# Small spacer loads ahead of each whole-tile store in a group normalization kernel

## The chip, the cores and the metric

The kernel runs on one core of one Trainium2 chip. The metric is device time in microseconds (us). Most executions agree within 0.3%. The kernel before takes 634.3 us.

Names: PE is the matmul engine, DVE VectorE, ACT ScalarE, POOL GpSimd, SP SyncE. SP does no arithmetic here: it issues nearly all DMA transfers. The transfers are carried out by 16 DMA engines; of the 128 packets of a tile, one per partition, each engine has 8. Its packets wait in its queue, also called its ring. A semaphore is a counter that one engine raises and another waits for.

## The reference

Group normalization over `x` of shape 128 x 1024 x 32 x 16 in bf16, with 32 groups, then a scale and a shift per channel:

```python
def reference(x, g, b):
    G = 32
    B, C, H, W = x.shape[0], x.shape[1], x.shape[2], x.shape[3]
    xr = x.reshape(B, G, C // G, H, W)
    mu = xr.mean(axis=(2, 3, 4), keepdims=True)
    var = ((xr - mu) ** 2).mean(axis=(2, 3, 4), keepdims=True)
    xn = (xr - mu) / jnp.sqrt(var + 1e-5)
    xn = xn.reshape(B, C, H, W)
    return xn * g[None, :, None, None] + b[None, :, None, None]
```

All of `x` has to be read once and all of the output written once: 134 MB each way.

## The kernel before

`x` is cut into 32 tiles of 128 partitions (4 images x 32 groups) by 16384 bf16, which is 32 KB per partition and 4 MB per tile. Six tiles are held on the chip. A tile is loaded, its mean comes from PE and DVE, its squares from ACT, then DVE, POOL and ACT scale it in place, and it is stored from the same buffer. The parts that matter here are the transfers, all on SP's queue:

```python
XBUFS = 6
UPFRONT = 6
AHEAD = 5
STORE_IN_PARTS = 2
...
    def L(i):                                    # load of tile i
        xt = xpool.tile([P, F], BF16, name="xt")
        parts = NQ if i == 0 or i >= NT - 1 else 1
        ...
            chain("sp", nc.sync.dma_start(out=xt[...], in_=x_v[i][...]))

    for i in range(min(UPFRONT, NT)):            # six loads at once
        L(i)
...
    def S(i, lo, hi):                            # store of tile i
        chain("sp", nc.sync.dma_start(
            out=o_v[i][:, lo * QF : hi * QF],
            in_=state[i]["xt"][:, lo * QF : hi * QF]))
...
    def finish(i):
        if i < 0 or in_parts(i):                 # the last two tiles are stored in quarters
            return
        for k in range(KC - LAST_SHARE, KC):
            scale_on("act", i, k)
        S(i, 0, NQ)
        state.pop(i)
        j = i + AHEAD
        if UPFRONT <= j < NT:
            L(j)                                 # waits until the store of tile i - 1 has landed
```

`chain` keeps the order on an engine. In steady state SP therefore issues, once per tile: a load as soon as an earlier store has freed a buffer, then the next store.

Of the kernel before, what the change touches and what calls it, by code (L numbers as in the profile page):

```python
# [11 lines left out]
BF16 = mybir.dt.bfloat16  # L12
# [10 lines left out]
STORE_IN_PARTS = 2  # L23
ACT_SHARE = 2
LAST_SHARE = 3
POOL_SHARE = 13


@with_exitstack
def kernel(  # L30
# [13 lines left out]
    nc = tc.nc  # L44
    P = nc.NUM_PARTITIONS
# [6 lines left out]
    NT = B0 // NS  # L52
# [11 lines left out]
    x_v = x.rearrange("(t n) (g k) h w -> t (n g) (k h w)", n=NS, g=G)  # L64
# [5 lines left out]
    xpool = ctx.enter_context(tc.tile_pool(name="xpool", bufs=XBUFS))  # L70
    jpool = ctx.enter_context(tc.tile_pool(name="jpool", bufs=1))
    spool = ctx.enter_context(tc.tile_pool(name="spool", bufs=4))
    pspool = ctx.enter_context(
        tc.tile_pool(name="pspool", bufs=2, space=bass.MemoryType.PSUM)
    )
# [9 lines left out]
    def chain(key, inst):  # L85
        prev = last.get(key)
        if prev is not None:
            tc.add_manual_dep(inst.ins, prev.ins.name, nosync, reason="pipeline order")
        last[key] = inst
        return inst  # L90
# [16 lines left out]
    for i in range(min(UPFRONT, NT)):  # L107
# [14 lines left out]
        out=eye[:],  # L122
        in_=ones_b[:],
# [8 lines left out]
        out=rep[:].rearrange("q (n a) -> q n a", n=NS),  # L132
        in_=ones_b[0:G, :].rearrange("q (n a) -> q n a", n=NS),
# [223 lines left out]
    def scale_on(key, i, k):  # L357
        st = state[i]
        span = st["xt"][:, k * HW : (k + 1) * HW]
        scl = st["scl"][:, k : k + 1]  # L360
        bia = st["bia"][:, k : k + 1]
        if key == "act":
            inst = nc.scalar.activation(  # L363
                out=span, in_=span, func=ACT.Identity, bias=bia, scale=scl
            )
        else:
            eng = nc.vector if key == "dve" else nc.gpsimd
            inst = eng.tensor_scalar(  # L368
                out=span,
                in0=span,  # L370
                scalar1=scl,
                scalar2=bia,
                op0=ALU.mult,
                op1=ALU.add,
            )
        chain(key, inst)

    def S(i, lo, hi):
        chain(
            "sp",  # L380
            nc.sync.dma_start(
                out=o_v[i][:, lo * QF : hi * QF],
                in_=state[i]["xt"][:, lo * QF : hi * QF],
            ),
        )

    def in_parts(i):
        return i >= NT - STORE_IN_PARTS

    def A(i):  # L390

        if not in_parts(i):
            for n in range(POOL_SHARE):
                scale_on("pool", i, KC - LAST_SHARE - POOL_SHARE + n)
            for k in range(KC - LAST_SHARE - POOL_SHARE):
                scale_on("dve", i, k)
            if i + 1 < NT:
                R1(i + 1)
            return
        for c in range(NQ):  # L400
            for k in range(c * KQ, (c + 1) * KQ):
                on_act = i == NT - 1 and k >= (c + 1) * KQ - ACT_SHARE
                scale_on("act" if on_act else "dve", i, k)
            S(i, c, c + 1)
            if c == NQ // 2 - 1 and i + 1 < NT:
                R1(i + 1)

    def finish(i):
        if i < 0 or in_parts(i):
# [7 lines that stand above are left out]
            L(j)  # L417
# [42 lines left out]
```

## Time and profile before

| | before |
|---|---|
| time | 634.33 us (634.23 to 634.92, 3 runs) |
| DMA, 60 to 560 us | share 1.00, 430 to 432 GB/s |
| ACT, the busiest compute engine | 85% of the span |
| load, store: issue to landing (medians) | 29.3, 38.3 us |
| a load and a store issued every | 19.4 us |

The page of the kernel before: the busy time of each engine; then the DMA's busy tenths in 40 equal slices of the span, the GB/s of those slices and the number of packets; then the DMA issues (transfer, engine, count, KB each, median us from issue to landing).

```profile
PE 293.1 (46%) x1025; PEld 114.4 (18%) x1025; DVE 380.2 (60%) x645; ACT 539.0 (85%) x268; POOL 346.8 (55%) x523
...
DMA  8999999999999999999999999999999999999996
GB/s 365 431 437 423 430 431 429 431 433 431 424 430 432 431 431 429 430 433 438 428 432 429 433 431 429 430 430 433 434 431 431 430 430 432 433 426 436 433 418 271
DMA packets 11063, 268.70 MB, mean 425 GB/s; under 512 B 1312, under 2 KB 1312, under 8 KB 1312
...
xt<-in_x_dram SPq DMA_DIRECT2D x30, 4096.0 KB, 29.3
out_dram<-xt SPq DMA_DIRECT2D x30, 4096.0 KB, 38.3
```

The strip of nines is the main reading: the DMA engines are busy in every slice but the ends, while no compute engine is. The busy time by window says the same of two inner stretches; its columns are the window, its length, then busy time and count of PE, PEld, DVE, ACT and POOL, the clock granted to PE, the DMA share and GB/s.

```profile
60.00:300.00 240.00, 111.30 (x386) 43.07 (x384) 159.00 (x256) 224.06 (x107) 151.60 (x226) 0.72 1.00 430
300.00:560.00 260.00, 120.55 (x416) 46.63 (x416) 160.81 (x259) 224.60 (x106) 155.61 (x232) 0.71 1.00 432
```

A busy DMA could still be short of work now and then. SP's timeline (start, length, engine, line, operation) and its longest waits (us in total, times, longest) show that it is not:

```profile
240.62 0.34 SPq L101 DMA_DIRECT2D xt<-in_x_dram  x1
241.06 0.37 SPq L381 DMA_DIRECT2D out_dram<-xt  x1
260.36 0.34 SPq L101 DMA_DIRECT2D xt<-in_x_dram  x1
260.81 0.37 SPq L381 DMA_DIRECT2D out_dram<-xt  x1
```
```profile
SPq L101 <- DMA out_dram<-xt: 425.4, 26, 19.0
SPq L381 <- DVE xt L368: 151.7, 18, 38.6
```

The load issued at 240.62 lands 29.4 us later (the median is 29.3), though its own 4 MB take 9.7 us: the load and the store issued one round earlier stand ahead of it, and land at 250.6 and 260.3. So in steady state about 20 us of work is queued. The 425 us that SP waits for stores to land is back-pressure from a full queue, not a loss.

The trace also records each DMA packet. A partition's 32 KB row of a tile is one packet. The records do not name the engine; packets that follow each other without a gap are taken to be of one. On one engine such packets start 1209 to 1210 ns apart, so 16 engines make 433 GB/s. After the eight packets of a tile comes one 4-byte packet that raises the semaphore, about 6 ns. All packets of the kernel add up to about 620 us per engine (480 x 1209.5 + 128 x 306 + 76 x 6 ns); the rest of the 632 us span is the start, stalls inside packets, and the tail.

### The profile page before, as it was taken

To read this page: it belongs to the slowest core of one execution; us is meant where nothing else is said; L and a number is where in the kernel's file an instruction comes from. 1 tells how busy PE (TensorE), PEld (TensorE's weight loads), DVE (VectorE), ACT (ScalarE), POOL (GpSimd) and SP (SyncE) were. 2 spreads that over 40 slices of the span, in tenths; PEclk is the share of its full clock that TensorE was granted. 3 is DMA by queue.
4 is the path that set the end of the run, shared out by engine and by line. 5 is a ranking of instruction groups with operands and counts; after the bars stand their busy time and mean duration, and the time that the engine had idled before them with its cause. 6 is when DMAs were issued, how large, how long until landed. Compare 5 with 4: busy or idle time off the path is not lost.

```text
span 631.9 us, 3907 instructions
## 1 busy us (share of the span) xinstructions
PE 293.1 (46%) x1025; PEld 114.4 (18%) x1025; DVE 380.2 (60%) x645; ACT 539.0 (85%) x268; POOL 346.8 (55%) x523
## 2 busy tenths in 40 slices
PE   5578604553245633456433565335553345647000
PEld 2233201221112211122111222112221112213000
DVE  1087666666676576545775457754657654577660
ACT  4589999999999897877997779977989797797960
POOL 0077666666666576544775446764557654477100
PEclk9689758766787657876678766677865788658655
DMA  8999999999999999999999999999999999999996
GB/s 365 431 437 423 430 431 429 431 433 431 424 430 432 431 431 429 430 433 438 428 432 429 433 431 429 430 430 433 434 431 431 430 430 432 433 426 436 433 418 271
DMA packets 11063, 268.70 MB, mean 425 GB/s; under 512 B 1312, under 2 KB 1312, under 8 KB 1312
## 3 DMA queue, kind: packets, MB, share of 16 engines
q1 hardware_dynamic: 10944, 268.44, 99.0%
q8 instruction: 8, 0.13, 0.1%
q14 instruction: 15, 0.12, 0.0%
q10 hardware_dynamic: 96, 0.00, 0.0%
HBM read 134.22 MB, written 134.22 MB: 425 GB/s over the span
## 4 chain that ended last, share of the span: by engine, by line
DMA 67%; ACT 15%; PE 7%; issue 4%; DVE 3%; POOL 0%; SPq 0%; DVEq 0%; ACTq 0%; POOLq 0%
DMA out_dram<-xt 42%; DMA xt<-in_x_dram 25%; ACT ja L244 13%; PE pa L166 7%; DVE xt L368 3%; ACT xt L363 2%; DMA gb_b<-in_g_dram 1%; POOL scl L337 0%; SPq L101 0%; ACT rstd L308 0%; DVE rstd L312 0%; DVE jd L189 0%; POOL shift L343 0%; DVEq L455 0%; DVE bia L324 0%
## 5 line engine op out<-in xcount | busy, mean ns | idle before, releaser
L244 ACT ACTIVATE ja<-xt,negmean 128x8192 fp8e5<-128x8192 bf16 x60 | 426.7, 7112 | 52.1 <-DVE jd L189 52.0
L166 PE MATMUL pa<-xt,eye 128*128 128x512 bf16 x976 | 281.8, 460 | 289.7 <-DMA xt<-in_x_dram 278.5
L368 DVE TENSOR_SCALAR xt<-xt,scl,bia 128x512 bf16<-128x512 bf16 x536 | 352.6, 732 | 40.0 <-POOL bia L353 40.0
L368 POOL TENSOR_SCALAR xt<-xt,scl,bia 128x512 bf16<-128x512 bf16 x390 | 308.7, 806 | 3.4 <-POOL bia L353 0.3
L166 PEld LDWEIGHTS <-eye 128*128 128x128 bf16 x1024 | 114.3, 114 | 468.5 <-DMA xt<-in_x_dram 290.6
L337 POOL TENSOR_SCALAR scl<-gb,rstd 128x32 f32<-128x32 f32 x31 | 11.2, 361 | 218.2 <-DVE rstd L312 218.2
L189 DVE TENSOR_SCALAR_CACHE_REDUCE jd<-pa 128x512 bf16<-128x512 f32 x32 | 22.0, 688 | 149.0 <-PE pa L166 149.0
L363 ACT ACTIVATE xt<-xt,bia,scl 128x512 bf16<-128x512 bf16 x98 | 72.0, 798 | 0.8 <-DVE bia L324 0.8
L244 ACT ACTIVATE ja<-xt,q 128x4096 fp8e5<-128x4096 bf16 x8 | 29.6, 3706 | 6.6 <-DVE jd L189 6.4
L312 DVE RECIPROCAL rstd<-rstd 128x1 f32<-128x1 f32 x32 | 5.1, 160 | 35.8 <-ACT rstd L308 35.8
L343 POOL TENSOR_SCALAR shift<-scl,negmean 128x32 f32<-128x32 f32 x31 | 11.2, 360 | 3.1
L216 POOL TENSOR_SCALAR off<-negmean,q 128x1 f32<-128x1 f32 x2 | 0.9, 432 | 20.5 <-DVE jd L189 20.5
L166 PE MATMUL pb<-xt,eye 128*128 128x512 bf16 x48 | 11.6, 388 | 1.0 <-DMA xt<-in_x_dram 1.0
L308 ACT ACTIVATE rstd<-s,v 128x1 f32<-128x1 f32 x30 | 8.8, 294 | 2.8
L244 ACT ACTIVATION_READ_ACCUMULATOR ja<-xt,negmean 128x1 f32 x60 | 11.2, 187 | 0.0
L353 POOL TENSOR_TENSOR bia<-shift,gb 128x32 f32<-128x32 f32 x31 | 7.8, 252 | 2.6
L308 ACT ACTIVATE rstd<-var,eps_t 128x1 f32<-128x1 f32 x2 | 0.6, 295 | 9.2 <-DVE jv L292 9.2
L273 POOL TENSOR_SCALAR v<-s 128x1 f32<-128x1 f32 x30 | 5.8, 192 | 2.5
L156 DVE COPY gb<-gb_p 128x64 f32<-128x64 f32 x1 | 0.2, 224 | 5.6 <-PE gb_p L148 5.6
L116 ACT ACT_TABLE_LOAD x1 | 1.3, 1283 | 1.7 <-PEq L444 1.7
L189 DVE DVE_READ_ACCUMULATOR jd<-pa 128x1 f32 x32 | 2.6, 81 | 0.0
L292 DVE TENSOR_SCALAR_CACHE_REDUCE jv<-sq,seed 128x4 f32<-128x4 f32 x2 | 0.4, 216 | 2.7 <-ACT ja L244 2.7
(18 smaller groups left out, 6.1 us busy)
## 6 DMA issues: line engine op xcount, KB each, us to landing
xt<-in_x_dram SPq DMA_DIRECT2D x30, 4096.0 KB, 29.3
out_dram<-xt SPq DMA_DIRECT2D x30, 4096.0 KB, 38.3
xt<-in_x_dram SPq DMA_DIRECT2D x8, 1024.0 KB, 16.5
out_dram<-xt SPq DMA_DIRECT2D x8, 1024.0 KB, 17.8
gb_b<-in_g_dram ACTq DMA_DIRECT2D x1, 2.0 KB, 3.2
gb_b<-in_b_dram ACTq DMA_DIRECT2D x1, 2.0 KB, 5.3
```

What stands on the lines that cost most here:

```text
L116: chain("act", nc.scalar.activation(out=warm[:], in_=eps_t[:], func=ACT.Sqrt))
L166: nc.tensor.matmul(out=ps[:], lhsT=eye[:], rhs=st["xt"][:, k * MMN : (k + 1) * MMN], start=(k == lo), stop=(k == hi - 1),),
L189: nc.vector.tensor_scalar(out=jd[:], in0=ps[:], scalar1=-inv_n, scalar2=seed, op0=ALU.mult, op1=ALU.add, accum_out=total[:],),
L244: nc.scalar.activation(out=ja[:, 0:w], in_=st["xt"][:, k * w : (k + 1) * w], func=ACT.Square, bias=bias, scale=scale, accum_out=sq, satura ...
L273: nc.gpsimd.tensor_scalar(out=v0[:], in0=s0[:], scalar1=inv_n, scalar2=EPS, op0=ALU.mult, op1=ALU.add,),
L308: nc.scalar.activation(out=rstd[:], in_=last_sum[:], func=ACT.Sqrt, bias=bias[:], scale=scale),
L312: chain("dve", nc.vector.reciprocal(out=rstd[:], in_=rstd[:]))
L337: nc.gpsimd.tensor_scalar(out=scl[:], in0=gam, scalar1=rstd[:], scalar2=None, op0=ALU.mult),
L343: nc.gpsimd.tensor_scalar(out=shift[:], in0=scl[:], scalar1=st["negmean"][:], scalar2=None, op0=ALU.mult,),
L353: nc.gpsimd.tensor_tensor(out=bia[:], in0=shift[:], in1=bet, op=ALU.add),
L363: inst = nc.scalar.activation(out=span, in_=span, func=ACT.Identity, bias=bia, scale=scl)
L368: inst = eng.tensor_scalar(out=span, in0=span, scalar1=scl, scalar2=bia, op0=ALU.mult, op1=ALU.add,)
```

## The change

The intent can be read from the names: a spacer in the queue between a load and the store behind it. The spacer is a load of 64 bytes per partition into a small spare buffer that nobody reads.

```diff
+GAP = 32
...
+    gappool = ctx.enter_context(tc.tile_pool(name="gappool", bufs=4))
...
+    def spacer():
+
+        room = gappool.tile([P, GAP], BF16, name="room")
+        chain("sp", nc.sync.dma_start(out=room[:], in_=x_v[0][:, 0:GAP]))
+
     def S(i, lo, hi):
+        if i < NT - STORE_IN_PARTS:
+            spacer()
         chain(
             "sp",
             nc.sync.dma_start(
```

It makes 30 more transfers, for tiles 0 to 29. The built program differs on SP alone. One side effect is not in the diff: the framework hands eight semaphores round among the transfers, and a transfer that gets a semaphore must wait until that semaphore's previous transfer has landed. With two transfers per tile a semaphore returns after four tiles; with three, after 2.7.

## The prediction

> **What bounds the kernel.** The DMA queue. In the page's 40-slice strip DMA is 9 except at both ends; the stage table (busy time by window) gives 430 to 432 GB/s from 60 to 600 us, while ACT, the busiest engine, has 85% of the span. The Trainium skill ("DMA: Bandwidth & Descriptors", Where 436 GB/s comes from) states a ceiling of 435.2 GB/s; the trace agrees: in its DMA packet records a 32 KB packet lasts 1213 ns and the next on that engine starts after about 1210, so 16 engines make 433 GB/s. A whole tile is 8 such packets per engine and one semaphore packet (about 6 ns), 9.68 us. All 76 transfers sum to about 619 us of packet time; the rest of the 632 us span is start, stalls and tail.
>
> The queue never runs dry. The timeline of SP shows a load and a store issued together every 19.4 us; the issue table has loads landing 29.3 and stores 38.3 us after issue (medians), so some 20 us of work is always queued. SP's 425 us of waiting for stores to land is back-pressure. Even the last store quarter, issued at 614.3 us, lands 17 us later.
>
> **What the change does.** Nothing on the compute engines. It adds 30 DMAs (tiles 0 to 29) of 128 packets of 64 bytes: 8 packets and one semaphore packet per DMA engine, between a load and a store in steady state.
> - Issue: 0.34 us each on SP, hidden by the backlog.
> - Semaphores: eight are handed round; with three DMAs per tile each returns after 2.7 tiles, not 4. In the built order a store now also waits for the load of two periods before, 39 us old and landed at 29: slack 10 us. In the tail, stores 27 and 28 wait some 5 us longer, with over 15 us still queued. No cost.
> - Engine time: the Trainium skill (same page, Queues, rings and completion order) says that each DMA engine consumes descriptors in ring order; the trace agrees (landings 9.7 us apart in issue order). So the packets are paid in full. 64-byte packets of the small loads on ACT's queue last 11 ns in the trace, semaphore packets 9 at a pitch of 6. Estimate: 8 x 8 + 6 = 70 ns per spacer, 2.1 us for 30. If their reads overlap badly, perhaps 0.3 us each, 9 us.
> - Stalls: time over 1213 ns in 32 KB packets totals 2.7 us per engine on average, about 6.5 on the worst, 1.9 of the 2.7 in the last two packets of a transfer, mostly loads just before a store; engines end between 623.4 and 630.5 us. A spacer could reduce this, at best by 3 to 5 us on the slowest engine; it may do nothing.
>
> **Prediction.** 634.3 + 2.1 + about 0.6 for imperfect overlap, stalls either way: 637 us, range 632 to 644. Faster by over 2% 0.01 (it would nearly go under the packet time), same 0.91, slower by over 2% 0.08.
>
> **Right if** DMA stays 9 in every inner slice, packets rise by 4320 (3840 of 64 bytes, 480 of 4), landings grow apart by about 0.1 us per spacer, compute groups keep their times and SP still waits mainly for stores to land.
>
> **Wrong if** small reads are exposed one after the other (0.5 us or more per spacer, 15 us and up), if semaphore reuse empties the queue (DMA slices below 9), or if the spacing removes stalls at load-to-store borders (mean 32 KB packet below 1218.7 ns, last landing earlier).

## The result, and the profile after

The changed kernel takes 636.27 us (635.68 to 636.66, 4 runs) against 634.35 us (634.23 to 634.92, 4 runs). The ratio is 1.0029, with a 95% interval from 1.0015 to 1.0043. A ratio here is the mean time of one kernel's runs over that of the other's of the same rounds, so it is not quite the ratio of the medians. The change costs 1.9 us by the medians (1.0 to 2.7 by the interval). That is far under 2%.

The page of the changed kernel, the same parts as before, with the issues of the spacer:

```profile
PE 285.6 (45%) x1005; PEld 113.1 (18%) x1025; DVE 379.2 (60%) x645; ACT 539.0 (85%) x268; POOL 345.4 (54%) x523
...
DMA  9999999999999999999999999999999999999995
GB/s 372 440 431 407 427 430 431 430 430 430 420 431 434 432 430 431 431 434 438 429 430 431 430 430 430 435 429 433 430 432 431 436 430 437 434 414 436 435 413 236
DMA packets 15383, 268.95 MB, mean 424 GB/s; under 512 B 5632, under 2 KB 5632, under 8 KB 5632
...
xt<-in_x_dram SPq DMA_DIRECT2D x30, 4096.0 KB, 29.3
out_dram<-xt SPq DMA_DIRECT2D x30, 4096.0 KB, 38.2
...
room<-in_x_dram SPq DMA_DIRECT2D x30, 8.0 KB, 29.1
```

There are 15383 - 11063 = 4320 more packets, all of them small: 30 x (128 + 16). (PE's busy time is no finding: some matmul records are missing, 1005 of 1025.) The spacer lands 29.1 us after its issue although it is tiny: it waits its turn in the ring, behind the load. The queue is as full as before. The busy time by window, and SP's timeline and waits:

```profile
60.00:300.00 240.00, 108.71 (x378) 42.58 (x384) 158.01 (x255) 223.99 (x108) 150.71 (x226) 0.73 1.00 429
300.00:560.00 260.00, 116.72 (x407) 46.21 (x416) 158.25 (x253) 221.96 (x105) 152.55 (x228) 0.74 1.00 431
```
```profile
240.58 0.33 SPq L103 DMA_DIRECT2D xt<-in_x_dram  x1
240.96 0.42 SPq L383 DMA_DIRECT2D room<-in_x_dram  x1
241.56 0.34 SPq L390 DMA_DIRECT2D out_dram<-xt  x1
```
```profile
SPq L103 <- DMA out_dram<-xt: 424.2, 26, 18.4
SPq L390 <- DVE xt L370: 124.1, 17, 37.6
...
SPq L390 <- DMA xt<-in_x_dram: 7.2, 1, 7.2
SPq L390 <- DMA out_dram<-xt: 6.7, 1, 6.7
```

The last two waits are new. They are the two stores near the end that now wait for a semaphore; each is one wait, and neither empties the queue. (The spacers themselves have two more new waits, 3.3 us in all.)

The packet records show what a spacer costs. This is one DMA engine at a load-to-store border (ns from the start, ns it took, bytes):

```
249846     9       4     semaphore of the load
249852    11      64     spacer, 8 packets, 7.1 ns from start to start
249859    11      64
249866    11      64
249873    11      64
249880    11      64
249887    11      64
249894    11      64
249902    11      64
249909     9       4     semaphore of the spacer
249914  1213   32768     first packet of the store
```

From 249852 to 249914 is 62 ns, and 30 such spacers are 1.9 us. There is no gap before, inside or after this one.

One formula gives all four data packet sizes. The Trainium skill ("DMA: Bandwidth & Descriptors", Where 436 GB/s comes from) has 32 bytes per cycle at 850 MHz on each port, which is 27.2 bytes per ns. The trace agrees: from 8 KB to 32 KB a packet grows by 24576 bytes and 903 ns. With four cycles (4.7 ns) added per packet, the start-to-start times are 7.06 ns for 64 bytes, 42.4 for 1 KB, 306 for 8 KB and 1209 for 32 KB. The records have 7.1, 42.4 (experiment e5), about 306 and 1209 to 1210. (The 4-byte semaphore packet is not covered: 4.9 by the formula, about 6 in the records.) That the extra is a number of cycles is an inference; its size is measured.

### The profile page after: what moved, and what is told of

It reads as the page before. It is cut to its first block, busy times and chain, and to the rows that moved or that the text cites. A ratio compares the mean times of both kernels' runs of the same rounds, so it can differ in the third digit from the quotient of the medians.

```text
span 634.8 us, 3942 instructions
## 1 busy us (share of the span) xinstructions
PE 285.6 (45%) x1005; PEld 113.1 (18%) x1025; DVE 379.2 (60%) x645; ACT 539.0 (85%) x268; POOL 345.4 (54%) x523
## 2 busy tenths in 40 slices
DMA packets 15383, 268.95 MB, mean 424 GB/s; under 512 B 5632, under 2 KB 5632, under 8 KB 5632
## 4 chain that ended last, share of the span: by engine, by line
DMA 62%; ACT 17%; PE 9%; issue 5%; DVE 3%; POOL 1%; SPq 0%; DVEq 0%; ACTq 0%; POOLq 0%
DMA out_dram<-xt 36%; DMA xt<-in_x_dram 26%; ACT ja L246 15%; PE pa L168 9%; DVE xt L370 3%; ACT xt L365 2%; SPq L103 0%; POOL scl L339 0%; POOL shift L345 0%; ACT rstd L310 0%; DVE jd L191 0%; DVE rstd L314 0%; SPq L383 0%; DVE jv L294 0%; DVEq L464 0%
## 5 line engine op out<-in xcount | busy, mean ns | idle before, releaser
L168 PE MATMUL pa<-xt,eye 128*128 128x512 bf16 x956 | 273.8, 453 | 299.7 <-DMA xt<-in_x_dram 297.9
L168 PEld LDWEIGHTS <-eye 128*128 128x128 bf16 x1024 | 113.0, 113 | 471.9 <-DMA xt<-in_x_dram 299.1
## 6 DMA issues: line engine op xcount, KB each, us to landing
room<-in_x_dram SPq DMA_DIRECT2D x30, 8.0 KB, 29.1
```

Source lines behind the costliest of these rows:

```text
L168: nc.tensor.matmul(out=ps[:], lhsT=eye[:], rhs=st["xt"][:, k * MMN : (k + 1) * MMN], start=(k == lo), stop=(k == hi - 1),),
```

## The experiments

The theory under test, called the packet theory: the DMA engines work through a queue that is always full, so the kernel pays for the packets of the spacers, each at bytes / 27.2 + 4.7 ns, and for nothing else. Its rivals: the cost is that of 30 more transfers (issue, semaphores, completion); or small reads have exposed latency; or, the border theory, a spacer at a load-to-store border eases stalls there, so that a larger cost is partly paid back.

"Over" below is the difference of the medians, in us, to the kernel before in the same rounds: 634.28 for e1 to e4, 634.47 for e5 to e8, 634.28 for e9 to e12. All kernels gave correct results.

| run | edit to the changed kernel | packet theory, us over | measured, us over | ratio (95% interval) |
|---|---|---|---|---|
| e1 | none | 1.9 | 1.6 | 1.0026 (1.0012 to 1.0039) |
| e2 | 1 packet per engine, not 8 | 0.4 | 0.9 | 1.0016 (1.0003 to 1.0029) |
| e3 | 32 packets per engine in one transfer | 7.0 | 5.6 | 1.0088 (1.0074 to 1.0102) |
| e4 | ahead of 26 loads instead | 1.6 | 1.1 | 1.0019 (1.0006 to 1.0032) |
| e5 | 1 KB per partition | 10.3 | 10.2 | 1.0162 (1.0147 to 1.0177) |
| e6 | four spacers per store | 7.5 | 7.0 | 1.0111 (1.0096 to 1.0126) |
| e7 | seven spacers per store | 13.1 | 83.8 | 1.1325 (1.1306 to 1.1343) |
| e8 | source on the chip | 1.9 | 1.4 | 1.0023 (1.0008 to 1.0038) |
| e9 | kernel before, again | 0 | -0.2 | 0.9993 (0.9979 to 1.0006) |
| e11 | issued from ACT | 1.9 | 1.7 | 1.0024 (1.0011 to 1.0036) |
| e12 | kernel before, 5 loads up front | 0 | 0.3 | 1.0001 (0.9987 to 1.0015) |

### e1: the changed kernel again

> Control: the changed kernel unaltered, on the same chip and in the same rounds as the next three. Packet theory (a DMA engine works through its packets in order, each costs its bytes at 27.2 B/ns plus about 4.7 ns, and the full queue hides all else): 30 x (8 x 7.06 + 5.9) ns = 1.9 us over the kernel before, ratio 1.003. All theories agree here; it sets the scale of noise.

Measured 635.91 us (635.70 to 636.10). The effect repeats on this chip, a little smaller.

### e2: one packet per engine

```diff
-        chain("sp", nc.sync.dma_start(out=room[:], in_=x_v[0][:, 0:GAP]))
+        chain("sp", nc.sync.dma_start(out=room[0:16, :], in_=x_v[0][0:16, 0:GAP]))
```

> The same 30 spacer DMAs, but on 16 partitions: one 64-byte packet per engine in place of eight; issues, semaphores and their reuse are as in the changed kernel. Packet theory: 30 x (7.06 + 5.9) = 0.4 us over the kernel before, about 634.7. Rival (the cost is that of 30 more transfers: their issue, semaphores taken out of the round, their completion): as the changed kernel, 1.9 us over, about 636.3.

Measured 635.15 us (634.86 to 636.02), between the two expectations; the interval (0.2 to 1.8 us) holds the packet theory's 0.4 us and e1's 1.6 us too. By the time alone this run decides little: the difference is as small as the scatter of single runs. The semaphore records help: each of the 16 engines raises the semaphore of the last store once. Averaged over the 16, this comes at 627.1 us of the span here, at 626.7, 626.5 and 626.6 in three profiles of the kernel before, and at 628.0 in e1. So with the same number of transfers most of the cost is gone once the packets are gone.

### e3: four runs of 64 bytes per partition

```diff
-        room = gappool.tile([P, GAP], BF16, name="room")
-        chain("sp", nc.sync.dma_start(out=room[:], in_=x_v[0][:, 0:GAP]))
+        room = gappool.tile([P, 4, 2 * GAP], BF16, name="room")
+        chain("sp", nc.sync.dma_start(
+            out=room[:, :, 0:GAP],
+            in_=x_v[0][:, 0 : 8 * GAP].rearrange("p (a b) -> p a b", a=4)[:, :, 0:GAP]))
```

> The same 30 spacer DMAs, each with four separate runs of 64 bytes per partition: 32 packets per engine in place of eight. Packet theory: 30 x (32 x 7.06 + 5.9) = 7.0 us over the kernel before, about 641.3. Rival of the transfers: 1.9 us, 636.3. A rival in which only bytes count (256 bytes per partition at 27.2 B/ns, 30 x 8 x 9.4) has 2.3 us, 636.6.

Measured 639.90 us (639.47 to 640.22), 5.6 over. This rules out both rivals named for it (1.9 and 2.3): the number of packets counts, with the same 30 transfers. It is also under the 7.0 us of the packet theory, and the interval (4.7 to 6.5 us) leaves 7.0 out. The packets do cost 7.0: the records have 15360 of them at 7.1 ns. Something gave about 1.4 us back; see "Stalls" below.

### e4: ahead of the load instead

```diff
     def L(i):
         xt = xpool.tile([P, F], BF16, name="xt")
+        if i >= UPFRONT:
+            spacer()
...
     def S(i, lo, hi):
-        if i < NT - STORE_IN_PARTS:
-            spacer()
```

> The spacer moved from ahead of each whole-tile store to ahead of each load from tile 6 on (26 of them), so it stands at the store-to-load borders. Packet theory: place is of no account, 26 x 62.4 ns = 1.6 us over the kernel before, about 635.9. Border theory (at its intended place a spacer pays back part of its cost by easing the stalls of a load's last packets ahead of a store): here nothing is paid back, so 3 us or more over. In the trace the packet theory expects the stalls of 32 KB packets (2.7 us per engine before, 2.4 in the changed kernel) to be anywhere in 2 to 3 us.

Measured 635.41 us (635.19 to 635.94), 1.1 over with 26 spacers. The border theory needed 3 us or more, which the interval (0.4 to 2.0 us) excludes. Place is of no account as far as the noise lets one see.

### e5: 1 KB per partition

```diff
-GAP = 32
+GAP = 512
...
-    gappool = ctx.enter_context(tc.tile_pool(name="gappool", bufs=4))
+    gappool = ctx.enter_context(tc.tile_pool(name="gappool", bufs=2))
```

> Spacer of 1 KB per partition (two spare buffers), same number of packets as the changed kernel, 16 times the bytes. Packet theory with its two terms: a packet costs 1024 / 27.2 + 4.7 = 42.4 ns, 30 x (8 x 42.4 + 5.9) = 10.3 us over the kernel before, about 644.7. If the cost goes with the number of packets or transfers alone: 1.9 us.

Measured 644.68 us (644.55 to 644.85), 10.2 over. Bytes count as well, at the engine's full rate.

### e6 and e7: four and seven spacers

```diff
-            spacer()
+            for _ in range(4):          # e7: range(7)
+                spacer()
```

The spare buffers are 16 in e6 and 28 in e7, so that a spacer never waits for its buffer first.

> Four spacer DMAs ahead of each whole-tile store (16 spare buffers), six DMAs per tile for eight semaphores. In the built order a spacer then waits for the load of the tile before, so the store is issued about 10 us after its load, with still some 10 us of work queued. Packet theory, with semaphore reuse hidden: 120 x 62.4 ns = 7.5 us over, about 641.8, DMA slices still 9. Rival (each transfer that takes a semaphore out of the round costs time of itself): more, 645 and up.

> Seven spacer DMAs ahead of each whole-tile store (28 spare buffers): nine DMAs per tile for eight semaphores, so that a store can be issued only when its own tile's preceding load has landed, and the queue must run dry there once per tile. Packets alone: 210 x 62.4 ns = 13.1 us, 647.4. Semaphore reuse is not hidden here: estimate 1 us from issue to first packet (first load: issued at 0.8 us, first packet at 1.8)[...], some 2 to 2.5 us in each of about 26 tiles, so 700 us in all, 690 to 720, and DMA slices below 9. If it comes out at 647, the backlog was not what hid the reuse.

e6 took 641.46 us (641.34 to 641.51), 7.0 over. Its DMA strip, SP's timeline and SP's two longest waits:

```profile
DMA  9999999999999999999999999999999999999995
```
```profile
241.86 0.33 SPq L103 DMA_DIRECT2D xt<-in_x_dram  x1
242.23 10.72 SPq L383 DMA_DIRECT2D room<-in_x_dram  x4
253.11 0.42 SPq L391 DMA_DIRECT2D out_dram<-xt  x1
261.55 0.33 SPq L103 DMA_DIRECT2D xt<-in_x_dram  x1
```
```profile
SPq L383 <- DMA xt<-in_x_dram: 253.1, 33, 11.0
SPq L103 <- DMA out_dram<-xt: 204.7, 26, 8.2
```

SP now waits 253 us in the middle of its spacers for semaphores, and issues the store 11 us after the load. It costs nothing: the strip is all nines, and the time is that of the packets.

e7 took 718.27 us (718.12 to 718.74), 83.8 over. The same views, with the busy time from 60 to 600 us:

```profile
DMA  9998898999989999899999999989999999998989
GB/s 381 439 431 364 343 392 360 355 410 385 379 342 373 410 382 383 358 355 407 356 385 356 382 384 381 383 329 410 376 362 383 356 408 357 376 390 328 413 348 388
```
```profile
254.38 0.34 SPq L391 DMA_DIRECT2D out_dram<-xt  x1
254.77 0.43 SPq L103 DMA_DIRECT2D xt<-in_x_dram  x1
255.24 11.70 SPq L383 DMA_DIRECT2D room<-in_x_dram  x7
276.42 0.34 SPq L391 DMA_DIRECT2D out_dram<-xt  x1
```
```profile
SPq L391 <- DMA xt<-in_x_dram: 250.6, 27, 10.2
SPq L383 <- DMA out_dram<-xt: 106.2, 26, 4.7
```
```profile
60.00:600.00 540.00, 220.10 (x758) 85.25 (x757) 300.92 (x481) 424.97 (x203) 288.80 (x430) 0.68 0.94 373
```

With nine transfers per tile and eight semaphores, the store of 276.42 waits for the load of 254.77 to land (27 waits, 250.6 us in all). By then nothing is queued. The DMA share falls to 0.94. The wait itself looks like e6's: 250.6 us against 253.1. What differs is whether work is queued while SP waits. The packet records split the 84 us: per engine, 13.1 us are the spacers' packets, 26.4 are longer 32 KB packets (29.1 us above their usual 1213 ns, against 2.75 before), and the rest, about 45, is idle time.

So 718 lies in the range, but partly by luck: the idle time is less than the 52 to 65 us that was expected, and the longer packets, whose cause is not known, were not foreseen. In the 18 rounds from 150 to 560 us the medians are 0.43 us from a load's last data packet to its landing, 0.08 to the issue of the store and 0.84 to the store's first packet.

### e8: the spacer's source on the chip

```diff
-        chain("sp", nc.sync.dma_start(out=room[:], in_=x_v[0][:, 0:GAP]))
+        chain("sp", nc.sync.dma_start(out=room[:], in_=ones_b[:, 0:GAP]))
```

> The spacer of the changed kernel, but copied from a constant that lies on the chip in place of the input in device memory: same packets, no reads of device memory. Packet theory: 1.9 us over, about 636.2. If part of the cost was the exposed latency of small reads from device memory: nearer to the kernel before, under 635.3.

Measured 635.88 us (635.58 to 636.04), 1.4 over; e1, on another chip, had 1.6. It is above the 635.3 that the rival named, though the interval (0.5 to 2.4 us) reaches down to it. The records decide: with no reads of device memory the 64-byte packets still start about 7 ns apart, so those reads cost nothing extra.

### e11: issued from ScalarE

```diff
-        chain("sp", nc.sync.dma_start(out=room[:], in_=x_v[0][:, 0:GAP]))
+        chain("act", nc.scalar.dma_start(out=room[:], in_=x_v[0][:, 0:GAP]))
```

> The spacer of the changed kernel issued from ScalarE's queue in place of SyncE's, so it stands in another ring of the same DMA engines and not between a load and a store, and SyncE issues what it did before. Packet theory: the engines pay for the packets wherever they come from, 1.3 to 1.9 us over, 635.6 to 636.2. Rival (its place in SyncE's queue, or SyncE's issue time, is what costs): as the kernel before.

Measured 635.96 us (635.80 to 636.80), 1.7 over. Another issuing engine and another ring leave the cost as it is. The spacers do get past part of the backlog there: they land 13.8 us after issue (median), against 29.1 on SP's ring, and each of the 30 lands before a transfer that SP had issued earlier. They are paid for all the same. The Trainium skill ("DMA: Bandwidth & Descriptors", Issuing engines are not separate DMA queues) says that DMAs of all issuing engines end up on the same 16 DMA engines; this run agrees.

### Stalls: e9, e10

> The kernel before, unaltered, for a second profile of it: how much do the stalls of its 32 KB packets vary from one execution to the next? If the 2.7 us per engine of the first profile is its own, and the 2.1 to 2.5 us in kernels with a spacer of eight or more packets per engine are an easing that spacers bring (border theory), this shows 2.6 us or more again. If they are noise, it may lie anywhere from 2.1 to 2.9. Time: as before, ratio 1.000.

> A third profile of the kernel before, for the same question: 2.6 us or more if spacers ease stalls, anywhere from 2.1 to 2.9 us if not.

e9 took 634.06 us (633.85 to 634.58). e10 is a single run of 635.01 us, state unknown, used for its profile. The time above 1213 ns in 32 KB packets, in us per engine, from one profile each:

| kernels | stall, us per engine |
|---|---|
| kernel before: first profile, e9, e10 | 2.75, 2.60, 2.79 |
| e12 (no spacers); e2 (one packet per engine) | 2.80; 2.82 |
| changed kernel, e1, e3, e4 | 2.40, 2.16, 2.14, 2.17 |
| e5, e6, e8, e11 | 2.48, 2.21, 2.14, 2.35 |

The two kinds don't overlap: with spacers of eight or more packets per engine the stalls are 0.2 to 0.6 us less than the mean of the three profiles of the kernel before (2.71), 0.3 in the changed kernel. (e7 is left out: its queue runs dry.) So the expectation that this was noise is the one that fell. But it is not the border theory as stated, since e4 and e11, whose spacers stand elsewhere, show the same. The first load-to-store border has 0.7 to 1.1 us in all kernels. The eased stalls lie from 100 to 300 us: 0.9 to 1.1 us there without spacers or with those of e2, 0.4 to 0.8 with the larger ones.

The easing fits the measured costs, which in e1, e4, e5, e6, e8 and e11 lie 0.1 to 0.5 us below the packet sum; the changed kernel's 1.9 us is the whole packet sum, so a single median doesn't show the easing. The mean over the 16 engines of the last store's semaphore shows it better. Against the 626.6 of the kernel before it comes later by 1.6 us in the changed kernel, 1.3 in e1, 6.3 in e3, 1.0 in e4, 10.2 in e5, 7.1 in e6, 1.2 in e8 and 1.4 in e11. Each is the packet sum less the easing, to within 0.15 us.

How small packets ease stalls is not known; it stays open. For e3 it explains 0.6 of the 1.4 us. The rest may lie in how far the slowest engine falls behind: its last semaphore comes 3.4 us after the mean of the 16 in e3, and 4.3, 4.9 and 5.7 us after in the three profiles of the kernel before. That is one profile of e3 and a spread as large as the rest itself, so it isn't shown.

### e12: a try for a faster kernel

```diff
-UPFRONT = 6
+UPFRONT = 5
```

This is the kernel before, without spacers.

> A try for a faster kernel, without spacers: five loads instead of six before the first store, so the first load-to-store border, where all profiles so far have 0.8 to 1.1 us of stall per engine, comes a tile sooner. Packet theory: the same packets, queue still full, so within 1 us of the kernel before; a gain of up to 1 us only if that first stall shrinks.

Measured 634.61 us (634.28 to 635.17), ratio 1.0001. The first stall did not shrink: it came a tile sooner, at 48 to 51 us, with 0.97 us per engine (0.83 to 0.91 in the three profiles of the kernel before), and the total is 2.80. With some 620 us of packets in a span of 632, little is left for any reordering.

## Why the prediction was right

- **The bound.** Right: the DMA queue is always full, and compute has no part in it. e7 shows the reverse case, in which it runs dry and the time goes up by 13%, of which the spacers' packets are 2 points.
- **Issue time hidden.** Right. A spacer's issue took 0.42 us, not 0.34, and moved nothing. e11 moves the issue to another engine at the same cost.
- **Semaphore reuse free.** Right, and for the reason given. The two stores near the end are issued some 9 us later than before (564.2 and 574.2 us against 554.5 and 565.4), not 5, of which 7 us each are the new waits; the DMA strip has nines there all the same. e6 waits 253 us and pays only for packets.
- **Packets paid in full, 70 ns per spacer, 2.1 us.** Right in kind, a little high: 62 ns and 1.9 us. The 8 ns pitch was read off packets that were not back to back; it is 7.1.
- **About 0.6 us for imperfect overlap.** Wrong, within the range: there is no gap in the records, and e8, without reads of device memory, costs as much as the others.
- **Stalls "either way".** They were eased by about 0.3 us per engine in the changed kernel, a sixth of the spacers' cost. So the last "wrong if" came half true: the mean 32 KB packet fell from 1218.7 to 1218.0 ns, but the last landing came later, not earlier (633.2 us against 631.0). The border as the place where a spacer has to stand, which the prediction considered, is refuted by e4 and e11.
- **The sum.** 637 was predicted and 636.27 measured. The surplus is the overlap term and the pitch; the low side of the range had to hold the easing. The range, 632 to 644, would also have held a gain of 2 us or the cost of e3, so hitting it proves little. The mechanism is confirmed by the signs: DMA slices of 9, 4320 more packets, unchanged compute, SP waiting mainly for stores, and store landings 19.60 us apart from tile 5 to tile 25 against 19.52.

## What to carry to other kernels

Before adding transfers or waits to a queue, find out whether it ever runs dry: compare the time from issue to landing with what one transfer takes by itself; the difference is the work that stands ahead of it. In this kernel it is always full, so waits of the issuing engine are free and every added packet is paid at nearly its full price, wherever it stands; if a wait outlasts the backlog, as in e7, the same wait costs far more than the packets. A transfer can also cost through the semaphores that it takes out of the round, and that is seen in the built order of waits, not in the diff.

## What the Trainium skill lacked or had wrong

- "DMA: Bandwidth & Descriptors", Why small descriptors are slow, has about 3 cycles of fixed overhead per packet. The runs fit 4 cycles of 850 MHz for 64 bytes to 32 KB: 7.1 ns for 64 bytes (3 cycles would be 5.9), 42.4 ns for 1 KB.
- The same page, Bandwidth, gives about 10.5 ns per packet from a 4 KB transfer issued from GpSimd. In a full queue fed from SyncE a 64-byte packet took 7.1 ns from start to start.
- The same page counts transfers under 64 KB as dominated by descriptors (Bandwidth), and here too only 19 of a spacer's 62 ns are its bytes. But it gives a fixed cost of about 2 us (Anatomy of one DMA, fitted for GpSimd's path). In a queue that is full an 8 KB transfer added 62 ns per DMA engine and no fixed cost beyond that; where the queue ran dry (e7), 1.35 us passed from the last data packet of a load to the first of the store behind it.
- The same page, Where 436 GB/s comes from, says that for transfers between HBM and SBUF the HBM side, about 358 GB/s, binds. As it stands the sentence does not hold here: this core alone ran at 430 to 432 GB/s, half reads and half writes, for 500 us. It lacks its condition, that the other core streams too, which the page's Bandwidth section does give.
- No page that was searched says what happens when a framework hands a few semaphores round among the transfers: eight of them for six transfers per tile cost nothing beyond the packets (e6), for nine per tile about 11% (e7, 718 us against 647 for its packets alone).
